# Two of batch 0's value chunks issued by ScalarE, first weights queued after the first scores, tile 0's stores ahead of GpSimd's value casts

## The chip, the cores and the metric

One core of a Trainium2 chip. The metric is the device time of one execution in microseconds (us).

## The reference

Windowed attention over 8 batches, 8 heads, 576 positions of 64, then a feed-forward layer over all 4608 rows:

```python
scores = scale * np.matmul(q, k.transpose(0, 1, 3, 2))      # q, k, v: (8, 8, 576, 64) f32
mask = np.abs(pos[:, None] - pos[None, :]) <= 32
attn = softmax(np.where(mask, scores, -1e9))
x = (attn @ v).transpose(0, 2, 1, 3).reshape(4608, 512)
h = x @ w_in                                                # w_in: (512, 2048)
out = gelu_tanh(h) @ w_out                                  # w_out: (2048, 512)
```

## The kernel before

The feed-forward part goes through the rows in tiles of 512 (t = 0, 1, ...) while the attention of the batch that comes next is woven into it. A kernel row such as `vr` or `wst` below is a staging buffer in f32; casts bring it into the f16 tiles `V`, `w_in16`. Two places matter.

The start. SyncE (SP) issues every load of batch 0 but two, then the values in chunks of 128 rows, then the first weights, all on its one queue:

```python
qk(0, (nc.sync, nc.scalar)); tails_0("k"); qk(2, (nc.scalar, nc.sync)); qk(4); qk(6)
load_table(exp_set)
vs(4, 0, 1, 2, 3)                       # values: the tail (4) and four chunks, on SP
wi = []
for i in range(4):                      # w_in: four buffers, two loads of 512 KB each
    wi.append(stage_w())
    for c0 in (0, 2):
        load_w_in(i, wi[i], c0, c0 + 2)
... # cut: masks, first scores, transposes (PE, DVE, ACT), casts of chunks 0 to 3,
    # attention times values, casts of w_in, first w_in matmuls
```

Tile 1. Four finished blocks of tile 0 wait in `later` as (block, buffer); two of them are halves of one buffer `yo2`, whose place (tag qt16) the cast of batch 2's query tails, `rest(0)` on ACT, takes next:

```python
for fc in range(begun, NF):
    ffn_in(t, fc)                                   # 4 matmuls with w_in, then a GELU on ACT
    if t == 1 and fc == 3:
        parts[0](); combine(4, nc.vector)           # batch 2: keys transposed, values loaded, by SP
    if t == 1 and fc in (5, 6):
        store(0, *later.pop(0), slice(0, 512), nc.scalar)
    if t == 1 and 6 <= fc < 10:
        cast_v(2, fc - 6)                           # GpSimd: waits for the values' landing
    if t == 1 and fc == 7:
        while later:
            store(0, *later.pop(0))                 # GpSimd
    if t == 1 and 9 <= fc < 14:
        parts[1](fc - 9)                            # rest(0..4), on ACT
```

The softmax here doesn't subtract the row's maximum and nothing guards it: scores larger than these inputs give would overflow.

Of the kernel before, what the change touches and what calls it, by code (L numbers as in the profile page):

```python
# [36 lines left out]
def cut(b):  # L37
    return 120 if b else 128
# [33 lines left out]
def kernel(  # L72
# [9 lines left out]
    nc = tc.nc  # L82
    B, H, S, D = q.shape
# [12 lines left out]
    def load_table(which):  # L96
        nc.scalar.add_instruction(mybir.InstLoadActFuncSet(  # L97
            name=nc.get_next_instruction_name(), act_func_set_id=which, ins=[], outs=[]))
# [29 lines left out]
    raws = {}  # L128

    def load_early(b):  # L130


        qr = rawp.tile([128, H, 256], FP32, name="qr")
        kr = rawp.tile([128, H, 256], FP32, name="kr")
        raws[b] = [qr, kr, None]

        def qk(h0, queues=(nc.sync, nc.sync)):
            for src, dst, queue in zip((q, k), (qr, kr), queues):
                queue.dma_start(
                    dst[:, h0:h0 + 2, :],  # L140
                    src[b, h0:h0 + 2, 0:512, :].rearrange("h (p j) d -> p h (j d)", j=4))

        def vs(*cs):
            if len(raws[b]) < 4:
                raws[b].append(stage.tile([128, 4, H, 64], FP32, name="vr", tag="stage"))
                raws[b].append(tailp.tile([64, H, 64], FP32, name="vt", tag="vt"))
            for c in cs:
                if c == 4:
                    nc.sync.dma_start(raws[b][4], v[b, :, 512:S, :].rearrange("h p d -> p h d"))
                else:  # L150
                    nc.sync.dma_start(raws[b][3][:, c, :, :],  # L151
                                      v[b, :, 128 * c:128 * c + 128, :].rearrange("h p d -> p h d"))

        def tails(which="qk"):
            if raws[b][2] is None:
                raws[b][2] = tailp.tile([128, H, 64], FP32, name="tr", tag="tr")
            tr = raws[b][2]
            if "q" in which:
                nc.sync.dma_start(tr[0:64, :, :], q[b, :, 512:576, :].rearrange("h s d -> s h d"))
            if "k" in which:  # L160
                nc.sync.dma_start(tr[64:128, :, :], k[b, :, 512:576, :].rearrange("h s d -> s h d"))

        return qk, tails, vs
# [41 lines left out]
    def stage_w():  # L205
        return stage.tile([128, 4, 512], FP32, name="wst", tag="stage")

    def load_w_in(i, w, c0=0, c1=4):
        nc.sync.dma_start(w[:, c0:c1, :], w_in_v[:, c0:c1, 512 * i:512 * i + 512])  # L209
        return w  # L210
# [10 lines left out]
    qk, tails_0, vs = load_early(0)  # L221
# [3 lines left out]
    qk(4)  # L225
    qk(6)
    load_table(exp_set)
    vs(4, 0, 1, 2, 3)
    wi = []
    for i in range(4):  # L230
        wi.append(stage_w())
        for c0 in (0, 2):
            load_w_in(i, wi[i], c0, c0 + 2)

    idle = KTs[1][:, 0, 0:512]
    nc.vector.memset(idle, 0.0)
# [19 lines left out]
    def blocks(copy, dst, src, r, *pieces):  # L256

        for p0, n, w, u in pieces:
            v0 = u + (8 if r == even else 24)
            copy(dst[r, :, p0:p0 + n * w].rearrange("k j (n p) -> k j n p", n=n),  # L260
                 src[r, :, v0:v0 + w].rearrange("k j (o p) -> k j o p", o=1).broadcast_to([64, 4, n, w]))
# [6 lines left out]
    for r in (even, odd):  # L268
        blocks(nc.vector.tensor_copy, bias[0], low, r, (0, 1, 24, 8), (24, 3, 32, 0), (120, 1, 8, 0))
        blocks(nc.scalar.copy, bias[1], low, r, (0, 1, 40, -8), (40, 2, 32, 0), (104, 1, 24, 0))  # L270
    nc.vector.memset(ones, 1.0)

    def band_out():
# [125 lines left out]
    def work_of(b, g):  # L399

        if g < 4:
            return (band[:, :, 0:120], [g], MAIN, SLOTS, 0, 120) if b else                 (band[:, :, 0:128], [g], MAIN_0, SLOTS_0, 0, 128)
        p0 = cut(b)
        return (band[:, :, p0:144], range(NPAIR), TAIL if b else TAIL_0, [(7, p0, 144)], p0, 144 - p0)

    def score(b, g, pair):
        m, prs, steps, slots, q0, n = work_of(b, g)
        ps = psS.tile([128, 2, 512], FP32, name="ps_s", tag=f"S{pair}")
        added = b == 0 and g < 4
        if added:  # L410
            for half in range(2):
                for h in range(2):
                    r0 = 64 * h
                    nc.tensor.matmul(ps[64 * half:64 * half + 64, h, :], idn[r0:r0 + 64, r0:r0 + 64],
                                     bias[half][r0:r0 + 64, :, :], start=True, stop=False,
                                     skip_group_check=True)
        for r, pr in enumerate(prs):
            for step in steps:
                for half, piece in enumerate(step):
                    if piece is None:  # L420
                        continue
                    k0, p0, p1 = piece
                    for h in range(2):
                        r0 = 64 * h
                        nc.tensor.matmul(  # L425
                            ps[64 * half:64 * half + 64, h, 4 * n * r:4 * n * r + 4 * n].rearrange(
                                "k (j p) -> k j p", j=4)[:, :, p0 - q0:p1 - q0],
                            KTs[b % 2][r0:r0 + 64, pr, k0:k0 + 64] if k0 < 512 else
                            KLs[b % 2][r0:r0 + 64, pr, :],
                            QTs[b][r0:r0 + 64, pr, :, p0:p1], start=not added, stop=True,  # L430
                            skip_group_check=added)
        w = 4 * n * len(prs)
        pe = yp.tile([128, 2, w], FP16, name="pe", tag="yo") if (b, g) == (1, 3) else \
            hp.tile([128, 2, w], FP16, name="pe", tag="qt16") if (b, g) == (0, 3) else \
            pep.tile([128, 2, w], FP16, name="pe", tag="pe") if g < 4 else \
            tailp.tile([128, 2, w], FP16, name="pet")
        nc.scalar.activation(pe, ps[:, :, 0:w], AF.Exp, scale=SCALE)  # L437
        groups[(b, g)] = pe
# [139 lines left out]
    def store(t, t4, yo, cols=slice(0, 512), *engs):  # L578

        m = i = 0  # L580
        while m < 128:
            b, c = divmod(t * 512 + t4 * 128 + m, S)
            q0, n = (0, cut(b)) if c < 4 * cut(b) else (cut(b), 144 - cut(b))
            j, p = divmod(c - 4 * q0, n)
            e = min(n - p, 128 - m)
            nj = 1 if p else max(1, min(4 - j, (128 - m) // n))
            eng = engs[i % len(engs)] if engs else nc.gpsimd
            if nj > 1:
                e = nj * n
                eng.dma_start(out_v[b, j:j + nj, q0:q0 + n, cols], yo[m:m + e, cols])  # L590
            else:
                eng.dma_start(out_v[b, j, q0 + p:q0 + p + e, cols], yo[m:m + e, cols])  # L592
            m += e
            i += 1

    later = []
# [80 lines left out]
    def turn(g):  # L677
        pts[g] = (bank16(0), bank16(1))
        trans_pair(0, g, *pts[g], now=False)
# [17 lines left out]
    spin(3)  # L697
    trans_tails(0, psO.tile([128, 8, 128], FP16, name="pt", tag="D"), odd, nc.scalar.copy)
    score(0, 0, 0)
    turn(1)  # L700
    cast_early(0, 2, split)
    trans_out(0, 1, *pts[1])
# [19 lines left out]
    qk, tails, vs = load_early(1)  # L722
# [80 lines left out]
    for t in range(NT):  # L803
        b = t + 1
        att = b < B
        if t:
            for fc in range(begun):
                ffn_in(t, fc, 3, 4, then=False)
            for fc in range(begun):
                gelu(t, fc)  # L810
            if att and b > 1:
                parts = cast_and_turn(b)
            for fc in range(begun, NF):
                ffn_in(t, fc)
                if t == 1 and fc == 3:
                    parts[0]()
                    combine(4, nc.vector)
                if t == 1 and fc in (5, 6):
                    store(0, *later.pop(0), slice(0, 512), nc.scalar)
                if t == 1 and 6 <= fc < 10:  # L820
                    cast_v(2, fc - 6)
                if t == 1 and fc == 7:
                    while later:
                        store(0, *later.pop(0))
                if t == 1 and 9 <= fc < 14:
                    parts[1](fc - 9)
                if t == 1 and fc == 8:
                    trans_tails(1, psO.tile([128, 8, 128], FP16, name="pt", tag="O"))
                if t > 1 and fc == 8 and att:
                    pair_v(b, nc.vector.tensor_copy)  # L830
# [10 lines left out]
        for i in range(113 if t else 65):  # L841
# [3 lines left out]
            for act in plan.get(i, "").split():  # L845
# [49 lines left out]
                elif kind == "v":  # L895
                    bb, gg = group(g)
                    o, d = weigh(bb, gg, at)
# [51 lines left out]
```

## Time and profile before

| | before |
|---|---|
| median of 4 runs (lowest to highest) | 313.83 us (312.45 to 314.51) |
| span of the profiled run, mean granted clock | 312.8 us, 0.984 |
| first matmul with w_in | 18.96 us |
| first matmul with w_out, tile 1 | 83.46 us |
| first exponential of the stage behind tile 1's w_in | 85.61 us |

Times inside a run count from the start of the span. The first row is what is judged; the other three are milestones on TensorE (PE) and ScalarE (ACT), and a change can be followed from one to the next.

### The profile page before, as it was taken

The page shows a single profiled execution, that of the slowest core. Times are in us where ns is not written, and L with a number is a line of the kernel's source. Part 1 is how long each engine was busy: PE and PEld are TensorE (multiplying, and loading weights), DVE is VectorE, ACT ScalarE, POOL GpSimd, SP SyncE. Part 2 cuts the span into 40 slices and gives each one's busy share as a digit, 9 for nine tenths or more (in the row PEclk, how much of TensorE's full clock was granted, in tenths as well). Part 3 has the DMA queues.
Part 4 walks back from the last instruction along what each step waited for, and adds up shares of the span by engine and source line. Part 5 has one row for each costly group of instructions (what it writes and reads, how often), then busy time and mean ns, then how long its engine had stood idle before and what let it go on. Part 6 is the DMA issues. An engine that isn't in the chain of part 4 may idle for free.

```text
span 312.8 us, 7121 instructions
## 1 busy us (share of the span) xinstructions
PE 291.1 (93%) x2894; PEld 179.9 (58%) x2894; DVE 194.3 (62%) x436; ACT 194.2 (62%) x307; POOL 90.8 (29%) x140
## 2 busy tenths in 40 slices
PE   7789799980999999999999999999999999999994
PEld 3544344430477448844884587458746874684583
DVE  4663557980395958586758677857785653542452
ACT  4866577641868578657766776677578747805600
POOL 3345426004060605050516042413250041006000
PEclk9999999997699999999999999999999999999999
DMA  7999999998199699989999999969899013004013
GB/s 219 228 340 373 322 280 263 249 224 195 24 250 144 119 168 229 149 138 144 217 160 201 120 243 142 185 131 221 112 132 152 2 30 107 2 0 135 2 34 101
DMA packets 116550, 50.73 MB, mean 162 GB/s; under 512 B 97911, under 2 KB 109943, under 8 KB 116518
## 3 DMA queue, kind: packets, MB, share of 16 engines
q1 hardware_dynamic: 87332, 37.88, 60.4%
q0 software_dynamic: 27776, 10.83, 24.7%
q10 hardware_dynamic: 1410, 1.58, 1.6%
q8 instruction: 22, 0.36, 0.6%
q14 instruction: 10, 0.08, 0.1%
HBM read 36.70 MB, written 9.44 MB: 147 GB/s over the span
## 4 chain that ended last, share of the span: by engine, by line
PE 66%; DMA 20%; SPq 7%; DVE 3%; POOL 1%; issue 1%; ACT 1%; DVEq 0%; ACTq 0%; POOLq 0%
PE mm L628 30%; PE mm L530 15%; PE ph L530 12%; DMA wst<-in_moe_w_out_dram 5%; DMA KT<-k 5%; DMA wst<-in_moe_w_in_dram 4%; PE ps_s L425 3%; SPq L175 2%; PE ps_d L448 2%; SPq L209 2%; SPq L151 2%; DMA tr<-in_k_dram 2%; PE ps_o L458 2%; DMA kr<-in_k_dram 2%; DMA qr<-in_v_dram 1%; DMA out_dram<-yo 1%
## 5 line engine op out<-in xcount | busy, mean ns | idle before, releaser
L530 PEld LDWEIGHTS <-w_in 128*128 128x128 f16 x576 | 56.7, 99 | 77.7 <-issue 12.5
L530 PE MATMUL mm<-xT,w_in 128*128 128x512 f16 x304 | 76.4, 386 | 9.2 <-ACT gT L538 9.1
L538 ACT ACTIVATE gT<-mm 128x512 f16<-128x512 f32 x76 | 45.1, 597 | 40.2 <-PE mm L530 39.5
L530 PE MATMUL ph<-xT,w_in 128*128 128x512 f16 x272 | 69.2, 383 | 0.2
L592 POOL DMA_DIRECT2D out_dram<-y x55 | 32.7, 603 | 87.6 <-DVE y L657 77.2
L573 DVE TENSOR_TENSOR s<-gT 128x512 f16<-128x512 f16 x64 | 26.9, 420 | 48.6 <-ACT gT L538 48.6
L628 PEld LDWEIGHTS <-s 128*128 128x128 f16 x512 | 49.4, 98 | 6.0
L538 ACT ACTIVATE gT<-ph 128x512 f16<-128x512 f32 x68 | 38.0, 600 | 15.0 <-PE ph L530 15.0
L628 PE MATMUL mm<-t,s 128*128 128x256 f16 x376 | 45.1, 273 | 0.0
L628 PEld LDWEIGHTS <-gT 128*128 128x128 f16 x384 | 36.0, 98 | 7.2 <-issue 0.6
L437 ACT ACTIVATE pe<-ps_s 128x960 f16<-128x960 f32 (+1 forms) x32 | 30.4, 975 | 11.8 <-PE ps_s L425 11.7
L628 PE MATMUL mm<-w_out,gT 128*128 128x256 f16 x256 | 33.6, 275 | 0.0
L97 ACT ACT_TABLE_LOAD x17 | 21.8, 1283 | 2.2 <-issue 1.9
L484 ACT ACTIVATE lt<-lt 128x480 f32<-128x480 f32 (+3 forms) x36 | 21.1, 585 | 1.1
L483 ACT ACTIVATE lt<-ps_d 128x480 f32<-128x480 f32 (+2 forms) x28 | 15.5, 555 | 9.0 <-PE ps_d L448 5.1
L443 DVE TENSOR_TENSOR pe<-pe,band 128x960 f16<-128x960 f16 x28 | 18.8, 695 | 1.2 <-ACT pe L437 1.2
L183 POOL DMA_DIRECT2D V<-in_v_dram x20 | 17.9, 910 | 1.1 <-issue 1.1
L458 PEld LDWEIGHTS <-V 128*64 128x64 f16 x520 | 13.9, 111 | 6.4 <-DVE V L200 2.6
L628 PE MATMUL mm<-t,gT 128*128 128x256 f16 x128 | 16.5, 273 | 0.0
L425 PE MATMUL ps_s<-QT,KT 64*64 64x128 f16 (+3 forms) x576 | 13.8, 216 | 0.8 <-DMA KT<-k 0.6
L628 PE MATMUL mm<-w_out,s 128*128 128x256 f16 x120 | 14.4, 273 | 0.0
L573 DVE TENSOR_TENSOR s<-s,gT 128x512 f16<-128x512 f16 x32 | 13.6, 425 | 1.1
(109 smaller groups left out, 320.5 us busy)
## 6 DMA issues: line engine op xcount, KB each, us to landing
kr<-in_k_dram SPq DMA_DIRECT2D x31, 256.0 KB, 10.9
qr<-in_q_dram SPq DMA_DIRECT2D x6, 1024.0 KB
wst<-in_moe_w_in_dram SPq DMA_DIRECT2D x8, 512.0 KB, 9.6
wst<-in_moe_w_out_dram SPq DMA_DIRECT2D x3, 1024.0 KB, 10.9
V<-in_v_dram POOLq DMA_DIRECT2D x20, 128.0 KB, 8.4
vr<-in_v_dram SPq DMA_DIRECT2D x8, 256.0 KB, 5.0
qr<-in_q_dram SPq DMA_DIRECT2D x7, 256.0 KB, 4.3
out_dram<-y POOLq DMA_DIRECT2D x6, 192.0 KB, 6.3
```

The costliest lines, as they stand in the source:

```text
L97: nc.scalar.add_instruction(mybir.InstLoadActFuncSet(name=nc.get_next_instruction_name(), act_func_set_id=which, ins=[], outs=[]))
L183: nc.gpsimd.dma_start(V[:, c, :, :], v[b, :, 128 * c:128 * c + 128, :].rearrange("h p d -> p h d"))
L425: nc.tensor.matmul(ps[64 * half:64 * half + 64, h, 4 * n * r:4 * n * r + 4 * n].rearrange("k (j p) -> k j p", j=4)[:, :, p0 - q0:p1 - q0], ...
L437: nc.scalar.activation(pe, ps[:, :, 0:w], AF.Exp, scale=SCALE)
L443: nc.vector.tensor_tensor(pe, pe, m.rearrange("k (o j) p -> k o j p", o=1).broadcast_to(list(pe.shape)), op=ALU.mult)
L458: nc.tensor.matmul(o[64 * h:64 * h + 64, cols].rearrange("d (j p) -> d j p", j=4)[:, :, p0 - q0:p1 - q0], Vs[b % 2][:, slot, 2 * pr + h, : ...
L484: nc.scalar.activation(lt[:, 0:n], lt[:, 0:n], AF.Exp, scale=-1.0)
L530: nc.tensor.matmul(ph, w_in16[:, dc, fc * 128:fc * 128 + 128], xT[:, dc, t * 512 % RING:t * 512 % RING + 512], start=(dc == 0), stop=(dc = ...
L538: nc.scalar.activation(gTs[t][:, fc, :], phs[fc], AF.Gelu_apprx_tanh)
L573: nc.vector.tensor_tensor(dst, x, y, op=op)
L592: eng.dma_start(out_v[b, j, q0 + p:q0 + p + e, cols], yo[m:m + e, cols])
L628: nc.tensor.matmul(pys["apart"][:, 0:256] if apart else py[:, blk, :], lhsT, wino[w][:, f, :], start=(new and i % (8 if one else 16) == 0) ...
```

## The change

Two intents. At the start: let ACT share the work of issuing, so that the queue of SP comes to the weights sooner. In tile 1: let GpSimd issue its stores before the casts that stand until batch 2's values land.

```diff
-    vs(4, 0, 1, 2, 3)
-    wi = []
-    for i in range(4):
-        ... load_w_in(i, wi[i], c0, c0 + 2)
...
         blocks(nc.scalar.copy, bias[1], low, r, ...)
+    vs(0, queue=nc.scalar)
+    vs(4, 1, 3)
...
     score(0, 0, 0)
+    vs(2, queue=nc.scalar)
+    wi = []
+    for i in range(4):
+        ... load_w_in(i, wi[i], c0, c0 + 2)
...
                 if t == 1 and fc in (5, 6):
                     store(0, *later.pop(0), slice(0, 512), nc.scalar)
+                if t == 1 and fc == 5:
+                    while len(later) > 1:
+                        store(0, *later.pop())
                 if t == 1 and 6 <= fc < 10:
                     cast_v(2, fc - 6)
-                if t == 1 and fc == 7:
-                    while later:
-                        store(0, *later.pop(0))
```

Below, part A is the stores and part B the values.

More of the change, by code (lines that the diff above doesn't have):

```diff
@@ L141, in qk, with vs @@
                     src[b, h0:h0 + 2, 0:512, :].rearrange("h (p j) d -> p h (j d)", j=4))
-        def vs(*cs):
+        def vs(*cs, queue=nc.sync):
             if len(raws[b]) < 4:
@@ L148, in vs @@
                 if c == 4:
-                    nc.sync.dma_start(raws[b][4], v[b, :, 512:S, :].rearrange("h p d -> p h d"))
+                    queue.dma_start(raws[b][4], v[b, :, 512:S, :].rearrange("h p d -> p h d"))
                 else:
-                    nc.sync.dma_start(raws[b][3][:, c, :, :],
-                                      v[b, :, 128 * c:128 * c + 128, :].rearrange("h p d -> p h d"))
+                    queue.dma_start(raws[b][3][:, c, :, :],
+                                    v[b, :, 128 * c:128 * c + 128, :].rearrange("h p d -> p h d"))
         def tails(which="qk"):
@@ L227 @@
     load_table(exp_set)
-    vs(4, 0, 1, 2, 3)
-    wi = []
-    for i in range(4):
-        wi.append(stage_w())
-        for c0 in (0, 2):
-            load_w_in(i, wi[i], c0, c0 + 2)
     idle = KTs[1][:, 0, 0:512]
@@ L699 @@
     score(0, 0, 0)
+    vs(2, queue=nc.scalar)
+    wi = []
+    for i in range(4):
+        wi.append(stage_w())
+        for c0 in (0, 2):
+            load_w_in(i, wi[i], c0, c0 + 2)
     turn(1)
```

## The prediction

> **What bounds the kernel now.** I first read the row of slices, to see where TensorE (PE) is not busy, then the waits of that stretch, then each engine's instructions in order of time. A slice is 312.8/40 = 7.82 us.
>
> ```profile
> PE   7789799980999999999999999999999999999994
> ACT  4866577641868578657766776677578747805600
> PEclk9999999997699999999999999999999999999999
> DMA  7999999998199699989999999969899013004013
> ```
>
> PE is full from slice 12 to the end: what is saved ahead of that should stay saved. It has one hole, slices 9 and 10 (62 to 78 us), where ACT falls too and PE's clock sags, and a looser start (slices 1 to 7). The waits of 60 to 80 us name the hole:
>
> ```profile
> POOL V L295 <- DMA qr<-in_v_dram: 17.3, 2, 16.5
> ...
> ACT qt L359 <- DMA out_dram<-yo: 9.9, 1, 9.9
> PE mm L530 <- ACT gT L538: 9.1, 1, 9.1
> ```
>
> PE waited 9.1 us for a GELU, ACT stood 9.9 us before a cast into qt, and it waited for a store of the output. In order of time (start, length, engine, line):
>
> ```profile
> 63.10 0.37 ACTq L592 DMA_DIRECT2D out_dram<-yo  x1
> 63.96 0.79 ACTq L592 DMA_DIRECT2D out_dram<-yo  x1
> 72.14 0.61 POOL L295 CAST V<-qr 128x512 f16<-128x512 f32 x1 [16.47 <-DMA qr<-in_v_dram]
> 73.62 0.61 POOL L295 CAST V<-qr 128x512 f16<-128x512 f32 x1 [0.87 <-DMA qr<-in_v_dram]
> 74.17 1.29 POOL L592 DMA_DIRECT2D out_dram<-yo  x2
> 77.23 0.62 ACT L359 CAST qt<-qt 16x512 f16<-16x512 f32 x1 [9.92 <-DMA out_dram<-yo]
> 78.39 3.57 PE L530 MATMUL mm<-xT,w_in 128*128 128x512 f16 x8 [9.12 <-ACT gT L538]
> ```
>
> The source tells why. Tile 0 leaves four blocks; two share one buffer (yo2, tag qt16), whose place the cast of the query tails takes next. One half of it was stored by ACT at 63.1. The other half was ready at 59.3 (a copy on DVE from 58.66, 0.68 long), but its store is a GpSimd (POOL) instruction behind two casts of batch 2's values, and those stand until the values land. So a ready store left at 74.17, landed 2.99 later (the chain of waits has it), and only then could ACT go on. POOL had been idle since 55.67 (last cast 55.06 + 0.61): nothing but its order of program made it late.
>
> The start (0 to 19 us) runs on two engines at once. POOL's casts wait for each landing, and ACT has no gap worth the name from 9.6 to 17.5:
>
> ```profile
> 7.21 0.61 POOL L288 CAST k<-kr 128x512 f16<-128x512 f32 x1 [1.91 <-DMA kr<-in_k_dram]
> 10.38 0.61 POOL L288 CAST k<-kr 128x512 f16<-128x512 f32 x1 [1.06 <-DMA kr<-in_k_dram]
> 15.84 0.61 POOL L295 CAST V<-vr 128x512 f16<-128x512 f32 x1 [1.68 <-DMA vr<-in_v_dram]
> 18.11 0.61 POOL L218 CAST w_in<-wst 128x512 f16<-128x512 f32 x1 [1.66 <-DMA wst<-in_moe_w_in_dram]
> 5.95 0.58 ACT L324 COPY KT<-pt 128x512 f16<-128x512 f16 x1 [1.17 <-PE pt L318]
> 16.95 0.60 ACT L743 CAST V<-vr 64x512 f16<-64x512 f32 x1
> ```
>
> **What the Trainium skill says.** (1) "PSUM — Partial Sum Buffer", section Engine vs sequencer instructions: the queues of ScalarE, VectorE and GpSimdE are strict FIFO. The trace agrees: the stores ready at about 59 left at 74.17, straight behind the second cast, on an engine idle for 16.47 us. (2) "TensorE: Matmul & The Clock Gate", What's actually happening: after about 3.4 us without work PE falls to half clock and needs about as long of work to recover. The trace agrees: granted clock 0.50 in each 2 us stretch from 74 to 84 us, 0.94 in the next, and matmuls 0.43 us apart in it against 0.22 before the hole. So the hole costs more than its 9.1 us. (3) "DMA: Bandwidth & Descriptors", Issuing engines are not separate DMA queues: issuing from a second engine saves only the time of issue; all run on the same 16 engines. (4) The same page, Why small descriptors are slow (HBM only): pieces of 256 bytes pay a fixed overhead. The value rows are 256 bytes. In 9 to 15 us, mostly values, the trace moved 214 GB/s with the DMA engines full, and 396 GB/s in 20 to 24, mostly first weights. So I do not expect a second queue to make the values cheap.
>
> **The change, part by part.** The order of instructions before and after shows no compute added or removed, on no engine; ACT's stream gains two issues and SyncE's (SP) loses two.
>
> Part A, the stores. Both GpSimd stores now stand ahead of the four casts. They can leave at about 58.2 and 59.4 (blocks ready at 58.19 and 59.34) and land, at 3 to 5 us each (3.0 in the hole, 4.8 for the busier ACT stores), by 64.5. ACT stores the other half of yo2 at 63.1 as before, landed by 67.9. ACT reaches the first tail cast after its GELU at 66.71 + 0.60 = 67.31, so it may stand 0.6 us instead of 9.92. I take 67.3 to 67.9 and work on from 67.4.
>
> Then ACT alternates five casts and six GELUs, at some 0.60 us each: 11 x 0.61 = 6.7, so its GELUs end near 74.1, the table load (1.28) near 75.4, where the first exponential starts. Before, that was 85.61: a gain of 10.2. PE: the 13th column needs the bank of a GELU ending near 68.6, the last one near 71.1, and 4 matmuls at 0.216 finish near 72.0, so w_out starts there (83.46 before, 11.5 earlier, of which about 12 x 0.21 = 2.5 is the regained clock). But 40 places later PE needs the masks behind those exponentials and batch 2's values: in the trace before from the first exponential to that point 89.63 - 85.61 = 4.0, so 79.4, where free PE would come at 72.0 + 5.5 = 77.5. A new wait of about 2 us takes part of 11.5 back: net 89.63 - 79.4 = 10.2.
>
> Is the rest there in time? The transposed keys were issued up to 68.45 and landed some 4 us later, 72.5; they are needed near 73, and by ACT not before 75.4. The values were cast by about 76.6 and then need about 1.1 of copying on DVE, 77.7 against 79.4. The 512 KB of stores now ride with batch 2's key load (58 to 63 us, DMA share 0.95 and more), which at 170 to 230 GB/s may push keys and values back by up to 2 us. That would cost up to 0.5. Part A: 9.7 to 10.2, say 10.0. Batch 3's loads follow the tail casts on SP; they move forward by some 8.5, less than 10, but its casts on DVE (103.2) had some 5 us to spare.
>
> Part B, the values. SP's eight value, tail and weight places move up by two, so the first weights may be issued near 9 instead of 12.02, and the last chunk of values should land near 14 instead of 17. Against it: each of ACT's two new issues carries a wait for an older landing in the order of instructions: chunk 0 for the second pair of keys (cast at 7.21), chunk 2 for the fourth pair (10.38). ACT is FIFO, so the KT copy of 5.95 slips to about 7.7 (7.2 + 0.5 of issue), the first exponential from 8.09 to 9.1, and chunk 2's issue at about 10.5 pushes the logarithm of 9.61 to 11.0. ACT is full from there: its cast of 16.95 slips to about 18.2, and PE's first w_in matmul from 18.93 to 19.5 or 20. Later PE waited 2.9 us in 17 to 68 us, mostly for DMA (1.5 of it for w_out's casts, the longest 1.2, about 36 us), and a late PE waits less there. The bytes that must have landed by then are the same. So B: between 1 us lost and 0.7 won; I take 0.2 lost.
>
> Sum: 314.35 - 10.0 + 0.2 = 304.55. As the hole's PE clock and some idle at 14 to 16 us (DMA share 0.83) may give a little more, I say 304.3.
>
> **The rivals.** *R1, the stall moves and does not go.* The casts of values are unblocked by nothing in this change: they still wait for landings near 72 and 73.6; if something that ACT or PE needs stood behind them, only 2 to 4 us would be won, time 310 to 312. For it: POOL's wait of 16.5 stays. Against: in POOL's order nothing else follows but the tail of the values and the next batch's loads. *R2, contention.* The early stores delay keys, then transposes, then values; a 3 us slip in all would leave 7 us, time 307.5. For it: full DMA there; against: 512 KB at the rate of the trace is 2.3 to 3 us if wholly exclusive, and there is slack of about 2. *R3, B decides.* If the ACT issues cost little and weights come 2 us earlier, the chain that runs through the loads up to 64 us moves too: 302. If ACT's late chain is passed on whole, 305.8. *R4, all of it hidden*: had PE not been full afterwards, no gain. Slices 12 to 38 speak against it.
>
> **Range and chances.** A alone gives 303.5 to 306, B adds -1.5 to +1.2, and three runs before scatter over 2 us (312.45 to 314.51). So 302.2 to 306.6. Faster by over 2% means below 308.1; only R1 or a strong R2 miss it: 0.93, within 2% 0.06, slower 0.01.
>
> **What would show it.** Right: POOL's two stores near 58 to 60 us, ahead of its long wait, which stays; ACT's wait for out_dram gone or below 1 us; no PE wait above 3 us in 60 to 90, clock 1.0 throughout; the first exponential near 75.4; everything from 100 us on as before, shifted by about 10. For B: ACT idle ahead of the KT copy until about 7.7, the last values by 14, first w_in matmul at 19 to 20. Wrong: PE at 68 to 80 standing for KT, values or gT again (R1, R2), or a first w_in matmul before 18 or after 20.5 (R3).

## More of the kernel before

A verdict says "faster" or "slower" when the time moves by over 2%.

A chunk of values is 128 partitions by 8 heads by 256 bytes; a load of `w_in` has rows of 2 KB.

The prediction shows the slices and waits; what it does not show is SP's order of issues at the start (start, length of the group, engine, line, what):

```profile
6.07 5.90 SPq L151 DMA_DIRECT2D vr<-in_v_dram  x4
12.02 6.25 SPq L209 DMA_DIRECT2D wst<-in_moe_w_in_dram  x8
```

All four value chunks are on the queue before the first weight.

## The result

| | before | after |
|---|---|---|
| median of 4 runs (lowest to highest) | 313.83 us (312.45 to 314.51) | 310.53 us (309.2 to 310.96) |
| span, clock | 312.8 us, 0.984 | 307.5 us, 0.982 |
| chunk 2 of batch 0's values cast | 15.84 us | 23.04 us |
| first matmul with w_in | 18.96 us | 27.72 us |
| first matmul with w_out, tile 1 | 83.46 us | 79.22 us |
| first exponential behind it | 85.61 us | 81.60 us |

The ratio of after to before is 0.9893, 95% interval 0.9844 to 0.9943: 1.1% faster, so within 2%, where 304.3 was predicted. Ratios here are the mean time of one kernel's fast runs over that of the other's in the same rounds, so not quite the ratio of the medians. Executions over 1.5% slower than the fastest of the same kernel are left out of the means.

The slices of the changed kernel (7.69 us each; tenths of busy time):

```profile
PE   7727999999999999999999999999999999999994
ACT  3770577857885787478747874787478757705600
PEclk9975999999999999999999999999999999999999
```

The hole at 62 to 78 us is gone: 9s, at full clock. But slice 3 (15.4 to 23.1 us) has PE at 2, where it had 8, and the clock falls to 7 tenths there and to 5 in the next slice. PE waits once from 17 to 66 us for more than 0.5 us:

```profile
PE mm L454 <- DVE V L200: 7.1, 1, 7.1
```

In order of time, GpSimd (POOL) and PE:

```profile
14.29 1.17 POOL L291 CAST V<-vr 128x512 f16<-128x512 f32 x2 [1.54 <-DMA vr<-in_v_dram]
23.04 0.62 POOL L291 CAST V<-vr 128x512 f16<-128x512 f32 x1 [7.58 <-DMA vr<-in_v_dram]
23.59 2.81 POOL L218 CAST w_in<-wst 128x512 f16<-128x512 f32 x4
25.03 0.43 PE L454 MATMUL mm<-pe,V 128*64 128x64 f16 x8 [7.12 <-DVE V L200]
...
66.02 0.74 POOL L588 DMA_DIRECT2D out_dram<-yo  x1 [10.47 <-ACT yo L604]
67.17 0.56 POOL L588 DMA_DIRECT2D out_dram<-yo  x1 [0.41 <-DVE yo L604]
```

Chunks 0 and 1 are cast at 14.29; chunk 2 lands so late that POOL stands 7.58 us. Four casts of w_in follow without a gap: the weights had landed and lay waiting behind values. The stores of part A do what they were moved for, at 66 us because the whole of tile 1 now starts 7.5 us late (65.18 for 57.66). And ACT no longer waits for them:

```profile
7.74 0.37 ACTq L151 DMA_DIRECT2D vr<-in_v_dram  x1
8.16 0.59 ACT L320 COPY KT<-pt 128x512 f16<-128x512 f16 x1 [3.38 <-DMA kr<-in_k_dram]
11.02 0.38 ACTq L151 DMA_DIRECT2D vr<-in_v_dram  x1
...
74.73 0.60 ACT L355 CAST qt<-qt 16x512 f16<-16x512 f32 x1
```

SP's issues, to be held against those of before:

```profile
5.86 3.66 SPq L151 DMA_DIRECT2D vr<-in_v_dram  x2
9.56 8.84 SPq L209 DMA_DIRECT2D wst<-in_moe_w_in_dram  x8
```

The first weights are 1.46 us ahead of chunk 2 (9.56 against 11.02); before, they were behind every value. The chain of waits goes straight through that chunk:

```profile
4.54 6.46 DMA kr<-in_k_dram
...
11.02 11.97 DMA vr<-in_v_dram
...
23.04 0.63 POOL V L291
```

A load completes with sixteen increments of a semaphore, one from each DMA engine. Their times below are starts of their transfer records; the semaphore shows each some 0.5 us later, the last at 22.99. The transfer records of the changed kernel, counted by queue (an ordinary listing; w_in rows are 2048 bytes on SP's queue, value rows 256 on ACT's):

```
us        w_in packets   chunk 2 packets   chunk 2 increments
15-16          49              720                7
16-17         135              144                8
17-18         182                2                0
18-19         187                7                0
19-20         190               11                0
20-21         186                9                0
21-22         183               11                0
22-23         189                4                1  (at 22.48)
```

Fifteen engines had finished by 16.61. The sixteenth came 5.9 us later, with only some 40 packets left to move. The w_in packets took 88 ns each and all sixteen engines did some 187 of them per us, about 12 an engine; the last engine's chunk moved 9 to 11 packets a us from 19 to 22. (Each record names its queue, not its engine; that it is one engine is read from the one missing increment.) Its packets come 0.106 us apart at the median, which is one value packet (19 ns) and one w_in packet (88 ns): on the engine with weights behind weights a small packet gets one turn for each large one.

One more record bears on this engine. The queue that the profile calls `q8 instruction` has one packet of 16 KB, from 16.53, 1.15 us long. Chunk 2's packets on the last engine stop at 16.53 and go on at 17.66, with 44 of its 64 still to move. So it was held for 1.1 us just when the others finished, and came back to a queue of weights. That both are one engine is read from these times. Only one of the four executions was traced, so it is not shown that the others were held too.

### The profile page after: what moved, and what is told of

The parts are those of the page before. It is cut to its first block, busy times and chain, and to the rows that moved or that the text cites. A ratio compares the mean times of both kernels' runs of the same rounds, so it can differ in the third digit from the quotient of the medians.

```text
span 307.5 us, 7117 instructions
## 1 busy us (share of the span) xinstructions
PE 289.8 (94%) x2894; PEld 180.3 (59%) x2894; DVE 194.7 (63%) x436; ACT 193.6 (63%) x307; POOL 87.8 (29%) x140
## 3 DMA queue, kind: packets, MB, share of 16 engines
q1 hardware_dynamic: 85252, 37.36, 59.4%
## 4 chain that ended last, share of the span: by engine, by line
PE 83%; DMA 7%; DVE 5%; ACT 2%; issue 1%; POOL 0%; ACTq 0%
PE mm L624 30%; PE mm L526 20%; PE ph L526 19%; DMA vr<-in_v_dram 4%; DMA kr<-in_k_dram 3%; PE ps_s L421 3%; PE ps_d L444 2%; PE mm L598 2%; PE py L598 2%; PE ps_o L454 2%; ACT gT L534 1%; PE ps_od L444 1%; DVE xT L489 1%; DVE s L569 1%; ACT qt L355 1%
## 5 line engine op out<-in xcount | busy, mean ns | idle before, releaser
L526 PE MATMUL mm<-xT,w_in 128*128 128x512 f16 x304 | 75.2, 380 | 0.1
L569 DVE TENSOR_TENSOR s<-gT 128x512 f16<-128x512 f16 x64 | 27.7, 432 | 37.3 <-ACT gT L534 37.3
L433 ACT ACTIVATE pe<-ps_s 128x960 f16<-128x960 f32 (+1 forms) x32 | 30.4, 976 | 10.4 <-PE ps_s L421 10.3
L421 PE MATMUL ps_s<-QT,KT 64*64 64x128 f16 (+3 forms) x576 | 13.9, 216 | 1.3 <-ACT KT L320 1.3
L421 PEld LDWEIGHTS <-KT 64*64 64x64 f16 x576 | 10.0, 106 | 7.4 <-issue 4.9
```

The source lines that it names most:

```text
L421: nc.tensor.matmul(ps[64 * half:64 * half + 64, h, 4 * n * r:4 * n * r + 4 * n].rearrange("k (j p) -> k j p", j=4)[:, :, p0 - q0:p1 - q0], ...
L433: nc.scalar.activation(pe, ps[:, :, 0:w], AF.Exp, scale=SCALE)
L526: nc.tensor.matmul(ph, w_in16[:, dc, fc * 128:fc * 128 + 128], xT[:, dc, t * 512 % RING:t * 512 % RING + 512], start=(dc == 0), stop=(dc = ...
L569: nc.vector.tensor_tensor(dst, x, y, op=op)
```

## The experiments

Theories, by the names that the expectations use. Where the missing 6 us went:

- **T1**: chunk 2 is late because the weights on the other queue are ahead of it; an engine takes turns between the queues.
- **R-A**: part A itself is worth little, and the values cost nothing.
- **R-B**: ACT's own work is late, because its issues carry waits and stand ahead of its copies and exponentials.
- **R-C / R-D**: the bytes ahead are what counts, whatever the turns; or two chunks on ACT's queue are too much for it.

Each kernel starts from before or after, as its diff tells. Of "before", 7 runs on the same chip each time: 314.28, 313.98 and 313.19 us for e1 to e4, e5 to e8, e9 to e11.

### e1: part A alone

```diff
 (after)
-    vs(0, queue=nc.scalar); vs(4, 1, 3) ... vs(2, queue=nc.scalar); w_in loads
+    vs(4, 0, 1, 2, 3); w_in loads          # where before has them
```

> Part A alone: the stores of tile 0 ahead of the casts, all value chunks on SyncE as before. The trace after has the start 7.5 us late (tile 1's first w_in matmul at 65.18 instead of 57.66) and yet the end 5.3 us early, so T1 (the start lost what part B cost, part A gave its whole gain) expects 313.8 - 7.5 - 5.3 = 301.0 us (300 to 303), ACT's wait for out_dram gone, first w_in matmul at 18.9 as before. My prediction's own sum for part A was 10.0, so 303.8. Rival R-A (part A gives only the 3 us seen, the late start is hidden by loads that decide anyway): 309 to 311.

Measured: 305.63 us (304.86 to 308.33), ratio 0.9731 [0.9669, 0.9792]: faster. The stores left at 58.29 and 59.45 (58.2 and 59.4 were worked out). What is left of the hole, in waits of ACT and of PE:

```profile
ACT qt L359 <- DMA out_dram<-yo: 3.4, 1, 3.4
PE mm L530 <- ACT gT L538: 2.6, 1, 2.6
```

So A works. The time lies between the 300 to 303 us of T1 and the 309 to 311 of R-A. The gain is 8.7, by the interval of the ratio 6.5 to 10.4, so the times alone do not exclude the prediction's 10.0. The trace shows what was left. The half of yo2 that ACT itself stores was issued at 62.89 and landed at 70.44, its data first moving at 67.2, where the prediction had it landed by 67.9; SP's transpose of the queries held SP from 61.26 to 66.4.

### e2: part B alone

```diff
 (after)
-                if t == 1 and fc == 5:  while len(later) > 1: store(0, *later.pop())
+                if t == 1 and fc == 7:  while later: store(0, *later.pop(0))
```

> Part B alone: chunks 0 and 2 on ScalarE, the stores as before. T1: the start is late by the same 7.1 us wait for chunk 2, and the hole stays because keys and values of batch 2 are loaded behind work of PE that is now late as well: 320 to 322 us. Rival R-A (start hidden behind loads): 313 to 315.

Measured: 317.69 us (316.4 to 320.31), ratio 1.0116 [1.0041, 1.0191]: B alone costs 1.16%, some 3.6 us, 2 to 4 less than T1 expected and more than R-A did. The start is that of the changed kernel, and the hole stays (ACT stood 8.9 us for the store). PE's waits up to 66 us, and POOL's late cast:

```profile
PE mm L454 <- DVE V L200: 7.3, 2, 6.3
```

```profile
21.78 0.61 POOL L291 CAST V<-vr 128x512 f16<-128x512 f32 x1 [7.01 <-DMA vr<-in_v_dram]
```

First w_in matmul 26.46, 7.5 us late, for 3.6 us at the end: about half of it is gone by then.

### e3 and e4: one chunk on ACT each

```diff
 e3 (after)                       e4 (after)
-    vs(4, 1, 3)                  -    vs(0, queue=nc.scalar)
+    vs(4, 1, 2, 3)               -    vs(4, 1, 3)
-    vs(2, queue=nc.scalar)       +    vs(4, 0, 1, 3)
```

> The changed kernel with chunk 2 back on SyncE ahead of the weights; chunk 0 stays on ScalarE. T1 (chunk 2 alone costs the 7 us, because it takes turns with the weights on another ring): last values cast by about 16 to 17, first w_in matmul at 19 to 20.5, time 301 to 303. Rival R-B (ACT held up by the waits that its two issues carry, first exponential 8.09 to 9.32, costs the most): the KT copy stays at about 8.2, chunk 0's wait stays, so 305 or more.

> The changed kernel with chunk 0 back on SyncE; only chunk 2 stays on ScalarE, issued after the first exponential while SyncE goes on to the weights. T1: chunk 2 is again cast late, at 20 us or later, PE waits 5 us or more for it, time 308 to 311. Rival R-B: the KT copy is back at 5.95 and ACT is late by 1 us at most, so 302 to 304.

Measured: e3 305.34 us (304.69 to 306.28), ratio 0.9708 [0.9664, 0.9753], as e1 within the scatter: chunk 0 on ACT, ahead of every weight, harms nothing (first w_in matmul 19.46, as T1 had it). e4 303.62 us (301.76 to 305.1), ratio 0.9648 [0.9592, 0.9705]. For e4 my expectation, late chunk and 308 to 311, was plainly wrong. Why, its issues show:

```profile
9.27 0.37 ACTq L151 DMA_DIRECT2D vr<-in_v_dram  x1
...
10.54 5.10 SPq L209 DMA_DIRECT2D wst<-in_moe_w_in_dram  x5
```

```profile
14.63 0.61 POOL L290 CAST V<-vr 128x512 f16<-128x512 f32 x1 [0.65 <-DMA vr<-in_v_dram]
```

In the first fence (ACT, then SP) chunk 2 is issued before the first weights; in the second POOL casts it at 14.63. Without chunk 0 ahead of them ACT's copies and the first exponential are earlier, SP has one chunk more before the weights, and chunk 2 is 1.27 us *ahead* of the first weight. All its increments came from 13.23 to 13.72. So "chunk 2 on ACT's queue" is not the cause by itself; I had misjudged which would be first. Both times lie in the ranges of R-B (305 or more, and 302 to 304) and not of T1; e6 tells the two apart.

### e5: the same bytes of weights in smaller rows

```diff
 (after)
-        for c0 in (0, 2):
-            load_w_in(i, wi[i], c0, c0 + 2)            # rows of 2 KB
+        for c0 in (0, 256):                            # rows of 1 KB, 512 KB a load as before
+            nc.sync.dma_start(wi[i][:, :, c0:c0 + 256], w_in_v[:, :, 512 * i + c0:512 * i + c0 + 256])
```

> The changed kernel, but each first-weight load takes 4 rows of 1 KB per partition instead of 2 rows of 2 KB; the same bytes, the same eight loads. T1 (turn by turn: on the engine that is late, each 256-byte packet of chunk 2 waits for one weight packet): in the changed kernel a 2 KB packet took 0.088 us and 41 packets of chunk 2 trickled out from 16.6 to 22.4 us; with 1 KB packets (0.046 us) the rest of chunk 2 needs about 60% of that, so its last increment comes near 19 to 20 instead of 22.5, the time near 307 to 309. Rival R-C (chunk 2 is served only when the weights are through, whatever their pieces): chunk 2 lands at 22 us or later and the time stays at 310 or above.

Measured: 305.9 us (303.81 to 306.7), ratio 0.9731 [0.9682, 0.978]. Same order of issues (weights 10.00, chunk 2 11.35), same bytes ahead; fifteen increments by 16.33, the sixteenth at 17.83 instead of 22.48:

```profile
18.59 0.61 POOL L291 CAST V<-vr 128x512 f16<-128x512 f32 x1 [2.78 <-DMA vr<-in_v_dram]
```

R-C (bytes count) wanted 22 or more and is refuted. Turns by packet predict the direction; the effect is larger than the 19 to 20 I had worked out. The packets say why: on the last engine chunk 2's come 0.064 us apart instead of 0.106 (w_in packets took 49 ns at the median), but there are only 24 of them from 16.36 on, and no pause: a `q8 instruction` packet (16.29, 1.17 us) ran beside them, so on another engine. An estimate from these spacings: for 44 packets the smaller rows save 44 x 0.042 = 1.8 us of the 4.65; the rest is that this engine was not held and had fewer left.

### e6: both chunks on ACT, close together

```diff
 (after)
-    vs(0, queue=nc.scalar)
+    vs(0, 2, queue=nc.scalar)
...
     score(0, 0, 0)
-    vs(2, queue=nc.scalar)
```

> The changed kernel with both chunks on ScalarE, but chunk 2 issued directly behind chunk 0, ahead of the KT copy, which is before SyncE comes to the weights (9.56). T1 in its second form (chunk 2 suffers only because it is issued after the weights are queued): values complete near 15 us, no long wait of PE, 303 to 306, ACT a little later at its start (KT copy 8.5 to 9). Rival R-D (two value chunks on the ScalarE queue are too much, or the two together delay it): chunk 2 cast at 20 us or later, 309 or more.

Measured: 303.94 us (302.65 to 305.32), ratio 0.968 [0.9635, 0.9725], as expected. The chunks go out at 7.00 and 8.49, weights from 8.78; all increments are there by 14.86. ACT is as late as in the changed kernel or later (its KT copy 8.91 for 8.16, PE waits 2.0 us for it), and it costs little (the wait, then POOL's cast of chunk 2):

```profile
PE ps_s L421 <- ACT KT L320: 2.0, 1, 2.0
```

```profile
15.64 0.61 POOL L291 CAST V<-vr 128x512 f16<-128x512 f32 x1 [1.17 <-DMA vr<-in_v_dram]
```

R-B and R-D are refuted: ACT late, two chunks on its queue, and no loss.

### e7 and e9: chunk 2 alone on ACT, later and later

```diff
 (e4)
     score(0, 0, 0)
-    vs(2, queue=nc.scalar)
...
     sums_of(0)
+    vs(2, queue=nc.scalar)             # e7
     cast_early(0, 3, split)
...
     score(0, 2, 0)
+    vs(2, queue=nc.scalar)             # e9, instead
```

> As the run with chunk 2 alone on ScalarE (303.6 us, chunk 2 issued at 9.27, ahead of the weights at 10.54), but its issue put behind the first logarithm and exponential, near 11 us, behind the first weights. T1 second form: chunk 2 lands late again, 18 to 23 us, PE waits 3 to 7 us, 306 to 310 us. Rival R-D: chunk 0 stays on SyncE, so nothing happens, 303 to 305.

> Chunk 2 alone goes from ScalarE, placed behind the exponentials of the third score, so issued near 13.2 to 13.8 us, while the first weights go out near 10.9, that is 2 to 3 us ahead of it (0.1 us ahead in the run before of this pair, where the sixteenth increment came at 16.4; 1.46 us ahead in the changed kernel, where it came at 22.5). T1 (a chunk counts as late from how far weights on the other queue are ahead of it, and on the engine with weights behind weights it gets one 256 B packet per 2 KB one): sixteenth increment at 20 to 24, more than 2 us behind the fifteenth, PE waits 4 us or more for chunk 2, first w_in matmul 24 to 28, and the time 305 to 309. If only the issue time counted (2.4 us later than in the run before): increments together by 17.5 to 19, PE waits 1 to 3 us, 304 to 305.

Measured: e7 304.0 us (303.36 to 305.88), ratio 0.9701 [0.9652, 0.975]; e9 305.96 us (305.09 to 306.72), ratio 0.9745 [0.9693, 0.9798]. Both missed T1's expectations (e7's late landing and 306 to 310; e9's sixteenth increment at 20 to 24 and wait of 4 us, where the longest was 2.0). e7 came out as R-D said, and e9's increments where "only the issue time counted" put them, though its time is in T1's range. Chunk 2 was moved less than I meant, since SP's weights came later as well (10.90, 11.41) and ACT's issue earlier than the place suggested (11.01, 12.13). In e9 the increments are spread, the first at 14.63, the fifteenth at 17.36, the sixteenth at 17.98: several engines late, none by much. In both runs the last engine's packets come 0.014 to 0.019 us apart, so they took no turns with weights.

### e10: the weights held until chunk 2 has landed

```diff
 (after)
     cast_v(0, 1)
+    wi = []
+    for i in range(4):
+        wi.append(stage_w())
+        if i == 0:      # a tiny copy that makes the first weights wait for chunk 2
+            nc.gpsimd.tensor_copy(wi[0][:, 0, 0:8], raws[0][3][:, 2, 0, 0:8])
+        ... load_w_in(i, wi[i], c0, c0 + 2)
```

> The changed kernel with one thing more: a tiny GpSimd copy from the landed chunk 2 into the first weight buffer makes the first weights wait for chunk 2. Everything else, the chunks' engines and their places included, is as in the changed kernel; chunk 2 is issued near 11.0 again. T1: with no weights in flight all sixteen increments come within 1 us of each other, by 14.6 to 15.6, and PE's wait for chunk 2 is gone (under 1 us); the weights start near 15.5 to 16.5 and land 4 to 5 us later than in the kernel with the stores alone, so the wait moves to w_in: first w_in matmul 21 to 24 (27.7 in the changed kernel, 19.8 with the stores alone), time 304.5 to 308. If ScalarE's queue were slow by itself from 11 us on, the sixteenth increment stays at 20 or later.

Measured: 308.27 us (307.37 to 310.33), ratio 0.9829 [0.9768, 0.9891], unclear by the rule of 2%; weights from 15.84 (all eight loads; chunk 2 was issued at 8.62).

```profile
15.63 0.19 POOL L720 COPY wst<-vr 128x8 f32<-128x8 f32 x1 [0.99 <-DMA vr<-in_v_dram]
15.76 0.61 POOL L291 CAST V<-vr 128x512 f16<-128x512 f32 x1
20.12 0.61 POOL L218 CAST w_in<-wst 128x512 f16<-128x512 f32 x1 [3.75 <-DMA wst<-in_moe_w_in_dram]
```

The sixteen increments came within 0.6 us (14.40 to 14.99), as T1 has it. The run is not the clean test that I meant: chunk 2 was issued at 8.62, not near 11, so its place moved too. And the time is at the top of the expected range: from 14 to 18 us the DMA engines were half idle (share 0.53 and 0.47), the first w_in matmul came at 20.79, and from the first load of w_out on (27.32 for 24.99) SP's loads were about 2 us later than in e1. Holding the weights gives the values back and loses loading time; by the intervals its time is not told apart from that of the changed kernel.

The start, run by run, in the order of how far the first weights were ahead of chunk 2 (us):

| run | first weights | chunk 2 | weights ahead by | sixteenth increment | issue to then |
|---|---|---|---|---|---|
| e10 | 15.84 | 8.62 | -7.22 | 14.99 | 6.4 |
| e4 | 10.54 | 9.27 | -1.27 | 13.72 | 4.5 |
| e6 | 8.78 | 8.49 | -0.29 | 14.86 | 6.4 |
| e7 | 10.90 | 11.01 | 0.11 | 16.37 | 5.4 |
| e9 | 11.41 | 12.13 | 0.72 | 17.98 | 5.9 |
| e5 (1 KB rows) | 10.00 | 11.35 | 1.35 | 17.83 | 6.5 |
| e2 | 9.09 | 10.54 | 1.45 | 21.21 | 10.7 |
| after | 9.56 | 11.02 | 1.46 | 22.48 | 11.5 |

Each row is one traced execution. Only the two kernels with rows of 2 KB ahead by about 1.45 us took over 6.5 us; up to 0.72 us ahead nothing is lost. But these two are also the two whose last engine was held by a `q8 instruction` packet in the middle of chunk 2 (in e2 from 15.94 to 17.14, its packets going on at 17.13), and the table can't part the two. Turns need no such holding: in e2 three engines that were not held moved their last packets some 0.1 us apart and were done at 16.89, 16.99 and 17.80.

### e8: both halves of yo2 stored by GpSimd

This run and the next ask why A alone gave 8.7 and not 10.

```diff
 (e4)
                 if t == 1 and fc == 5:
-                    while len(later) > 1: store(0, *later.pop())
+                    for x in (0, 2): store(0, *later[x])                      # yo2's halves, GpSimd
                 if t == 1 and fc in (5, 6):
-                    store(0, *later.pop(0), slice(0, 512), nc.scalar)
+                    store(0, *later[{5: 1, 6: 3}[fc]], slice(0, 512), nc.scalar)
```

> As the run with chunk 2 alone on ScalarE (303.6 us), but the two early GpSimd stores are the two halves of the shared buffer yo2, and ScalarE stores the two other blocks. That run still had ACT waiting 4.3 us for ScalarE's own store of a half of yo2, issued at 61.1 and landed at 69.6. If that landing is what is left of the hole, the first tail cast starts at 65.3 instead of 69.6, PE's wait of 3.5 us goes below 1, and the time is 299 to 301. If something else ends there at the same time (the tails' own load, batch 2's keys), the gain is below 1.5 us.

Measured: 302.16 us (302.07 to 305.23), ratio 0.9646 [0.9591, 0.9701], the lowest median of all, though by ratio the same as e4, and short of the 299 to 301 expected. The profiled run is the slowest of the four (305.23; the others 302.07 to 302.23), so what follows may not hold for the median. ACT's wait before qt is gone (cast at 65.30) and the first exponential comes at 72.17, 5 us ahead of e1's. In this run a new wait takes it back (waits of DVE and PE, then POOL in order of time):

```profile
DVE V L192 <- POOL V L290: 3.4, 1, 3.4
...
PE ps_od L453 <- DVE V L193: 2.9, 1, 2.9
```

```profile
74.59 0.61 POOL L290 CAST V<-qr 128x512 f16<-128x512 f32 x1 [16.30 <-DMA qr<-in_v_dram]
```

Batch 2's values are now what ends last.

### e11: batch 2's values loaded by GpSimd instead

```diff
 (e8)
-                for c in range(4):                    # in keys(), behind the keys' transposes
-                    nc.sync.dma_start(vr[:, c, :, :], ...)
-                if t == 1 and 6 <= fc < 10: cast_v(2, fc - 6)
+                if t == 1 and fc == 6: load_v(2)       # GpSimd DMA, cast on the way
```

> The run with both halves of yo2 stored by GpSimd (302.2), and batch 2's values no longer loaded by SyncE behind the keys' transposes and cast by GpSimd, but loaded and cast in one by GpSimd's own DMAs right behind its early stores, as later batches' values are. If the values' place at the end of SyncE's stream is what took the gain of that run: the four loads go out at 59 to 63, land by 72, the wait of VectorE for V (3.4) and of PE behind it (2.9) go, first exponential of the next stage 72 to 73 as there, and the end comes 2 to 4 us earlier: 298 to 300.5. If something else holds that stage (the keys' transposes, the vector engine's own work): same as there, 301.5 to 303.

Measured: 307.76 us median of 5 runs (306.92 to 313.14), ratio of the four fast ones 0.979 [0.9713, 0.9866]: against before unclear by the rule of 2%, against e8 worse, and outside both of my ranges. The profiled run is the slowest of the fast ones (311.04); its waits:

```profile
PE ps_s L416 <- DMA KT<-k: 6.5, 1, 6.5
```

The wait for V is gone and one for the keys has come. SP's two issues of the keys' transposes, in e8 and then in e11:

```profile
64.98 5.01 SPq L370 DMA_TRANSPOSE KT<-k  x2
```

```profile
66.16 7.75 SPq L370 DMA_TRANSPOSE KT<-k  x2
```

They held SP 7.75 us instead of 5.01 (2.6 to 5.0 in all runs without this), with the values' loads under way. So moving the values only moves the wait; that these loads are what delays the keys is likely, but no run shows it alone. In all the other runs with part A the end of the span comes some 223 to 225 us after batch 2's last value cast ends (e1 79.91 and 303.1, e8 78.09 and 303.5, e9 79.75 and 303.8, e10 82.02 and 306.1, after 84.35 and 307.5); before, it was 236 (76.63 and 312.8). That is a coincidence of times and proves no cause, but with e8 and e11 it says what comes next when the hole is closed: batch 2's keys and values.

## Why the prediction was wrong

**Part A, mechanism right, size off by 1.3, which is inside e1's interval.** The working gave 10.0; e1 gave 8.7. POOL's stores left when worked out and the wait of 9.9 fell. Mis-sized was "landed by 67.9" for ACT's own store of half of yo2: it landed at 70.44, so ACT waited 3.4 us and not 0.6. Rival R2, contention, is the part of the text that had this, at up to 0.5 us. The keys' transposes on SP moved from 65.35 to 67.01 and the values' loads from 68.50 to 70.85. Removing that wait as well (e8) gave little; in the run that was traced batch 2's loads then end last. (The sum starts from 314.35, the median of the three runs known then; a fourth makes it 313.83. And 18.93 is the load of weights into PE ahead of the first w_in matmul, which is at 18.96.)

**Part B, the step that failed.** It is "the last chunk of values should land near 14 instead of 17", and with it "so B: between 1 us lost and 0.7 won". Chunk 2's sixteenth increment came at 22.48. (Chunk 3, which stayed on SP, did land earlier, 15.36 for 16.50 by its semaphore.) The times of issue were right: KT copy 8.16 for "about 7.7", first exponential 9.32 for 9.1, chunk 2 11.02 for 10.5, logarithm 11.44 for 11.0, weights 9.56 for 9. What failed is the inference from a place on a queue to a landing. I took SP's places moving up by two as gain for all that followed and forgot that chunk 2 had left that queue: it lost its place ahead of 4 MB of weights. "The bytes that must have landed by then are the same" is true of the total and false of the order.

I had cited "Issuing engines are not separate DMA queues" from the Trainium skill's page "DMA: Bandwidth & Descriptors" for what a second issuing engine does not gain, and not asked what it loses. Two other sections of the same page have what was lacking. "Queues, rings and completion order" says that each DMA engine goes round between the queues it has work for, packet by packet. The trace agrees within its reach: on the last engine 9 to 11 packets of 256 bytes a us against some 12 of 2048, one every 0.106 us, and every 0.064 us in e5 with the large ones halved. "Why a DMA increments its semaphore by 16 and not by 1" says that the engines finish independently and only the full sixteen mean landed. The trace agrees: fifteen by 16.61, the last at 22.48. What the prediction could not have is the `q8 instruction` packet that held this engine for 1.1 us (before had one from 12.61); whether chance or the later start put it there, no run shows.

What followed from it is shown step by step: PE stood 7.1 us, restarted at half clock (0.50 from 20 to 30 us), the first w_in matmul came 8.8 us late, w_out 7.6, tile 1 7.5. From there to tile 1's w_out the closed hole won 11.8 (57.66 to 83.46 before, 65.18 to 79.22 after), where the prediction had 11.5. Together 4.2 at that point and 5.3 at the end of the span (the two profiled runs; 3.3 between the medians).

**The sum.** A was worth -8.7 (e1) and B +3.6 (e2), -5.1 together; the two at once gave -3.3. By ratio, after is 1.7% over e1, some 5 us, so B may cost more once A is in; but each of these ratios has an interval of some 2 us either way, so that is not shown. R3 ("B decides") was the right rival with a range too small, 305.8 at worst, because it only counted ACT's late chain. The text's own sign of R3 was a first w_in matmul after 20.5; it came at 27.72.

**What stays open.** How much of B's loss is the order of the queues alone. Shown are the turns (spacing 0.106, and 0.064 with half the row) and, over four runs each, that B's loss comes with chunk 2 behind 2 KB rows and goes when it is ahead (e4, e6) or the rows are halved (e5). Not shown is whether it would be as large without the packet that held the last engine in both traced executions, nor whether the untraced ones had it. Open too: why only 49 w_in packets moved in 15 to 16 us, though five loads had been issued by 13.9, which let the other fifteen engines drain chunk 2; and why one engine was already some 0.8 us behind the others in nearly all loads from 2.10 us on (1.2 in e5, 0.4 or less in e2).

**The better version.** Part A with the values as before gives 305.6; with chunk 2 alone on ACT, behind the first exponential (e4), 303.6; with both halves of yo2 stored by GpSimd besides (e8), 302.2. All three are faster than before by over 2%, and 1.6 to 2.5% below after; between e4 and e8 the scatter does not decide.

## What to carry to other kernels

Before a load is moved to another engine's queue, list what was behind it on the old one: order on one queue was a priority that nothing in the program names, and on two queues small rows take turns with large ones. A transfer is as late as its last DMA engine, so look at the sixteenth increment and not at the mean rate. And when a hole is closed, look up at once what would have come next there (here batch 2's keys and values): it sets how much of the hole can be won.

## What the Trainium skill lacked or had wrong

- "DMA: Bandwidth & Descriptors", "Queues, rings and completion order": it gives some 9 to 17 descriptors as typical for a packet. The records here show packets of one row each, 256 bytes for values and 2048 for w_in, at 19 and 88 ns. The page does not draw the consequence that a load of small rows is slowed by the row size of another queue: on the last engine one value packet every 0.106 us beside 2 KB rows, every 0.064 beside 1 KB.
- The same page, "Issuing engines are not separate DMA queues": that a second issuing engine saves only time of issue leaves out that it gives up the order. Chunk 2 took 4.5 us when issued 1.27 us before the weights and 11.5 when 1.46 us after (1.1 of it the pause for the `q8 instruction` packet).
- The same page, "Why a DMA increments its semaphore by 16 and not by 1": no size is given for how far the engines may be apart. Here, from the first increment to the last, 0.5 us (e4) to 6.7 (after) for the same load.
- No page that I read says how transposing loads fare beside GpSimd's casting loads: two of them held SP 7.75 us and landed 11.5 us after their issue with those under way (e11), 2.6 to 5.0 and 3.2 to 6.1 in the runs without.
- No page that I read says that a packet of the queue `q8 instruction` keeps a DMA engine from the data of the others: here one of 16 KB held the last engine from 16.53 to 17.66.
